# A spectral filter beside a gated dense block on one core: VectorE's own results in the planner, one chunk's dense part ahead of forward tiles, accumulating transfers moved to other sums

## The chip, the core and the metric

The kernel runs on one core of a Trainium2 chip. Work is issued on TensorE (PE in the profile), VectorE (DVE), ScalarE (ACT), GpSimd (POOL, here only a queue that issues accumulating DMAs) and SyncE (SP, the queue of all other DMAs). The metric is the device time of one execution in microseconds (us), as the median of several runs; one further execution was profiled.

## The reference

`x` is 2048 x 512 (the second input `B_x` of the same shape is not used; both parts read `A_x`). Everything is float32.

```python
g = sigmoid((x * gate_w).sum(-1, keepdims=True))          # one gate per row
X = rfft2(x, axes=(-2, -1)) * (w_r + 1j * w_i)            # filter in the frequency domain
a = irfft2(X, s=(2048, 512), axes=(-2, -1))
h = gelu(x @ w1 + b1)                                     # 512 -> 1792
b = h @ w2 + b2                                           # 1792 -> 512
out = g * a + (1 - g) * b
```

## The kernel before, in words

Every product on TensorE is made in split precision: an operand is stored as a rounded high part (suffix `h`) and the remainder (suffix `l`), and a product takes three matmuls, high by high, high by low, low by high. The high part is a copy on ScalarE. The remainder comes in one of two ways: VectorE subtracts the high part from the source (`split`), or ScalarE writes the negated high part into the low buffer and a DMA issued by GpSimd adds the source onto it in place (`minus`, `acc`). VectorE's subtraction of a 128x512 tile and the accumulating DMA of 256 KB are thus two prices for the same thing.

The work falls into these stages:

- **Forward, 16 tiles** (`forward(j)`, rows j, j+16, ...). Per tile: folds on VectorE (`eo`, `w`), a split (`eoh`, `eol`), eight matmuls into `pd`, another split into `zb` buffers (`zb0`/`zb2` high, `zb1`/`zb3` low, used in turn), six matmuls into `py` with a table `tf` loaded for each tile, and a rearrangement into the spectrum `y` by way of `pys`. The gate's logits come out of `pd` as well.
- **Dense block, four chunks of 512 rows, in two halves of the hidden units** (`mlp(half, c)`). Per hidden tile f: twelve 512-wide matmuls into `ph` (names `ph<chunk>_<f>`), gelu on ScalarE, a split into `g<chunk>_<f>h` and `...l`. Then four output tiles `po<half>_<chunk><q>` of 21 matmuls each. Half 0 (f from 0 to 6) stores its sums with the bias in a DRAM buffer `bacc`; half 1 (f from 7 to 13) adds to it. Before the change, chunk 0 of half 0 writes gelu's result to an SBUF tile `gst`, from which ScalarE makes both the high part and the negated one, and an accumulating DMA the low part. The two PSUM tiles that `ph` may hold at a time are then free as soon as gelu has read them.
- **Filter** (`stage1`, `own_rows`, `filt`, `stage4`): radix-4 steps over the 16 tiles and the product with the filter `wf`, almost all on VectorE. `own_rows` sends two rows of the spectrum through DRAM (`ywas`, `own`, `yfix`) and TensorE (`pown`) and comes before the first filter step, whose tiles are `b0d`, `b0s`.
- **Inverse** (`inverse(c, h, late)`): per tile a twist on ScalarE and VectorE (`sw`, `pq`), a split `v`, matmuls into `pz`, a split into `zb`, matmuls into `pa`, then `od`, `u`, `v`, `w`. For the chunks in `LATE` (3 and 0) half 1 of the dense block is already in `bacc`, added there by accumulating DMAs; `inverse` loads it as `ba`, multiplies by the gate and subtracts it from `w` on VectorE before the store. For chunks 1 and 2 the last sum is made in `last`.

The order of the instructions on each engine is fixed when the program is built. `Graph.schedule` is a list planner: each step has an engine, a cost, a lag until its result is there, and a rank, and at each moment the free engine takes the ready step of the lowest rank for which buffers are free. For steps of the same engine (`own`) the planner counts the result as there when the engine is free again, with no lag. `turn_of(n)` is the rank 0.8 + 0.01 n; `EARLY` is 0.5, `FEED` is 1. Forward tiles have ranks from 0.80 to 0.95 in the order `NORD` = 0, 4, 8, 12, 1, 5, ..., 11, 15; tile 15 is the last.

Of the kernel before, what the change touches and what calls it, by code (L numbers as in the profile page):

```python
# [12 lines left out]
F32R = mybir.dt.float32r  # L13
# [42 lines left out]
def _tables():  # L56
# [123 lines left out]
class Graph:  # L180
# [45 lines left out]
    def schedule(self):  # L226
# [123 lines left out]
def tile_kernel(ctx: ExitStack, tc: tile.TileContext, xt, xc, w1, w2, b1, b2, x0g, wf, wrev, out, consts):  # L350
# [204 lines left out]
    def load_mx(half, c):  # L555
        if (half, c) == (1, 3):
            X[half, c] = X[0, 3]
            return
        X[half, c] = new_x(half, c)
        if half == 0:  # L560
            h, l = X[0, c]
            for q in range(NQ):
                def part(b, q=q):
                    return b.ap()[:, q].rearrange("p a b -> p (a b)")

                x = buf("xm", [P, 4 * P], F32, f"xm{c}{q}")
# [12 lines left out]

    def forward(j):  # L580
# [54 lines left out]
        def segs(t, c, lo, step):  # L635
            o = t.ap()[:, c, lo:lo + P]
            return bass.AP(tensor=o.tensor, offset=o.offset, ap=[list(o.ap[0]), [step, 2], list(o.ap[1])])

        for c in range(2):
            a(lambda c=c: act.activation(segs(xh, c, 0, P + c), segs(ps, c, P, P + 4), AF.Copy), 256, [(ps, c)], [(xh, c)], 0)  # L640
# [201 lines left out]
    def inverse(c, h, late):  # L842
# [76 lines left out]
        for k, op in enumerate((ALU.add, ALU.subtract)):  # L919
# [9 lines left out]
            if late:  # L929
                v(lambda w=w, k=k: vec.tensor_tensor(w.ap(), w.ap(), ba[k].ap(), op=ALU.subtract), 512, [ba[k]], [w])  # L930
# [14 lines left out]
    def load_w(n, f):  # L945
# [5 lines left out]
        a(lambda: act.activation(h.ap(), t.ap(), AF.Copy), 512, [t], [h], rank)  # L951
        if f < FA and (n == "a" or f < 0):
            v(lambda: vec.tensor_tensor(l.ap(), t.ap(), h.ap(), op=ALU.subtract), 512, [t, h], [l], rank)
# [3 lines left out]
    def mlp(half, c):  # L957
# [7 lines left out]
        for f in fs:  # L965
# [25 lines left out]
            else:  # L991
                m(up, 512, 12, [*W["a", f], *xx], [ps])
            if half == c == 0:
                t = buf("gst", [P, 512], F32, f"gs{c}_{f}")
                h, l = G[f] = [buf("hid", [P, 512], F32R, f"g{c}_{f}{k}") for k in "hl"]
                rank = 0.9 if half else FEED if c else EARLY
                a(lambda f=f, ps=ps, t=t: act.activation(t.ap(), ps.ap(), AF.Gelu_apprx_tanh, bias=b1t.ap()[:, f:f + 1]), 600,
# [7 lines left out]
            if half and c == 2:  # L1005

                v(lambda ps=ps: vec.scalar_tensor_tensor(ps.ap(), gb.ap()[:, c], 1.0, ps.ap(), op0=ALU.subtract, op1=ALU.mult),
                  512, [gb], [ps], 0.9)
            G[f] = split(f"g{c}_{f}", "hid", [P, 512], ps, lambda x: x, 512, 0.9 if half else FEED if c else EARLY)
        for q in range(NQ):  # L1010
# [16 lines left out]
            for n in (slice(0, 2 * P), slice(2 * P, 4 * P)) if end else (slice(0, 4 * P),):  # L1027
# [142 lines left out]
```

## Time and profile before

| | us |
|---|---|
| median of 3 runs (lowest, highest) | 390.63 (390.21, 390.88) |
| the profiled execution | 391.24 |
| its span, first to last instruction | 389.4 |
| TensorE busy, 1839 matmuls | 374.5 (96%) |
| VectorE busy, 743 instructions | 340.5 (87%) |
| ScalarE busy, 421 instructions | 229.8 (59%) |
| granted TensorE clock | 1.00 |

The profiled execution took 1.84 us more than its span, and 0.61 us more than the median of the runs. Busy time is the union of an engine's instructions. A matmul's record overlaps the next one's, so that short waits between matmuls do not show as idle time: of TensorE's waits the table above shows a part.

### The profile page before, as it was taken

The numbers are of one execution on the slowest core, as the hardware profiler recorded it, in microseconds if no ns is written. First come the engines' busy times: TensorE is split into PE (matmuls) and PEld (weight loads), VectorE is DVE, ScalarE is ACT, GpSimd is POOL, SyncE is SP. The second block draws the span as 40 slices with busy tenths as digits, with TensorE's granted clock in tenths as the row PEclk, the third lists the DMA queues.
The fourth block names the chain that finished last, engine by engine and source line by source line (L and its number), as shares of the span: only waits on it lengthen the run. The fifth ranks groups of instructions, "written<-read, shape, count | busy, mean of one in ns | idle before, by whom it ended". The sixth has DMA issues, their size and how long they took to land.

```text
span 389.4 us, 5547 instructions
## 1 busy us (share of the span) xinstructions
PE 374.5 (96%) x1839; PEld 311.6 (80%) x1839; DVE 340.5 (87%) x743; ACT 229.8 (59%) x421; POOL 32.3 (8%) x52
## 2 busy tenths in 40 slices
PE   8898899999999999999999899999999999998996
PEld 7777788788888888888887677887888878887885
DVE  4999999999998999999979967786979799899962
ACT  4999986688552532375396495379419994045300
POOL 0122320000000000012043002000110000000000
PEclk9999999999999999999999999999999999999999
DMA  8998999966483235669299335416243065610321
GB/s 275 346 279 176 252 241 286 368 213 210 148 264 113 81 135 155 174 162 247 83 247 167 85 159 93 63 36 228 35 63 27 8 222 174 212 43 0 114 105 54
DMA packets 41189, 61.72 MB, mean 158 GB/s; under 512 B 4576, under 2 KB 19488, under 8 KB 40384
## 3 DMA queue, kind: packets, MB, share of 16 engines
q1 hardware_dynamic: 35832, 51.67, 40.2%
q0 software_dynamic: 5184, 9.44, 15.7%
q10 hardware_dynamic: 144, 0.26, 0.3%
q8 instruction: 14, 0.23, 0.2%
q14 instruction: 15, 0.12, 0.1%
HBM read 42.60 MB, written 16.92 MB: 153 GB/s over the span
## 4 chain that ended last, share of the span: by engine, by line
PE 38%; DVE 30%; ACT 19%; DMA 8%; issue 4%; SPq 0%; DVEq 0%; ACTq 0%
PE po L419 20%; PE ph L419 12%; ACT sw L858 4%; DVE m L817 4%; DMA wf<-in_wf 2%; DVE y L721 2%; ACT ph L1003 2%; PE pa L419 2%; DMA bb<-bacc 2%; PE pd L419 2%; ACT sw L861 2%; ACT y L673 2%; DMA ti<-ti 1%; PE pz L419 1%; PE py L419 1%
## 5 line engine op out<-in xcount | busy, mean ns | idle before, releaser
L1003 ACT ACTIVATE ph<-ph,b1t 128x512 f32<-128x512 f32 x49 | 32.1, 656 | 36.6 <-PE ph L419 36.5
L1040 ACT ACTIVATE o<-po,b2t 128x512 f32<-128x512 f32 x16 | 10.9, 691 | 28.5 <-PE po L419 24.9
L858 ACT ACTIVATE sw<-y,al 64x512 f32<-64x512 f32 x32 | 23.1, 723 | 2.6 <-DVE y L721 2.0
L817 DVE TENSOR_TENSOR m<-y,wf 128x514 f32<-128x514 f32 x32 | 20.7, 689 | 0.2
L419 PE MATMUL py<-zb,tf 128*128 128x258 f32 x96 | 17.7, 297 | 3.3 <-ACT pys L666 1.2
L419 PEld LDWEIGHTS py<-zb,tf 128*128 128x128 f32 x96 | 14.3, 189 | 6.5 <-ACT pys L666 1.8
L884 ACT ACTIVATE zb<-pz 128x512 fp32r<-128x512 f32 x16 | 9.4, 592 | 13.5 <-PE pz L419 13.5
L865 DVE SCALAR_TENSOR_TENSOR pq<-y,al,sw 128x256 f32<-128x256 f32 x32 | 14.1, 479 | 3.2 <-ACT sw L861 3.1
L673 ACT ACTIVATE y<-pys 64x257 f32<-64x257 f32 x32 | 13.4, 418 | 4.4 <-DVE pys L670 4.0
L419 PEld LDWEIGHTS pa<-zb,ci 128*128 128x128 f32 x96 | 13.2, 189 | 2.8 <-ACT zb L884 1.6
L419 PE MATMUL pa<-zb,ci 128*128 128x256 f32 x96 | 14.4, 286 | 0.3 <-ACT zb L884 0.2
L642 DVE TENSOR_TENSOR zb<-pd,zb 128x256 fp32r<-128x256 f32 x32 | 12.1, 419 | 2.3 <-ACT zb L640 1.9
L885 DVE TENSOR_TENSOR zb<-pz,zb 128x512 fp32r<-128x512 f32 x16 | 11.0, 685 | 3.0 <-ACT zb L884 3.0
L410 POOL DMA_DIRECT2D bacc<-o x8 | 7.0, 876 | 75.3 <-ACT o L1043 53.0
L593 DVE TENSOR_TENSOR w<-eo 128x256 f32<-128x256 f32 x32 | 12.8, 419 | 0.3
L419 PE MATMUL pd<-cf,eoh 128*128 128x254 f32 (+1 forms) x64 | 10.9, 290 | 1.7 <-ACT eoh L598 1.7
L590 DVE TENSOR_TENSOR eo<-xf 128x256 f32<-128x256 f32 x32 | 12.3, 419 | 0.0
L646 DVE TENSOR_TENSOR zb<-zb,pd 128x256 fp32r<-128x256 f32 (+1 forms) x32 | 11.9, 412 | 0.4
L600 DVE TENSOR_TENSOR eol<-w,eoh 128x512 fp32r<-128x512 f32 (+1 forms) x17 | 11.1, 655 | 1.0 <-ACT eoh L598 1.0
L598 ACT ACTIVATE eoh<-w 128x512 fp32r<-128x512 f32 (+1 forms) x17 | 10.2, 600 | 2.9 <-DVE w L593 2.8
L887 DVE TENSOR_TENSOR zb<-zb,pz 128x512 fp32r<-128x512 f32 x16 | 11.0, 686 | 0.4
L419 PEld LDWEIGHTS pd<-cf,eoh 128*128 128x128 f32 x64 | 9.2, 189 | 2.6 <-ACT eoh L598 1.9
(574 smaller groups left out, 1292.9 us busy)
## 6 DMA issues: line engine op xcount, KB each, us to landing
wf<-in_wf SPq DMA_DIRECT2D x16, 257.0 KB, 3.5
tf<-tf SPq DMA_DIRECT2D x16, 256.0 KB, 5.4
bacc<-o SPq DMA_DIRECT2D x16, 256.0 KB, 3.4
xf<-in_xt SPq DMA_DIRECT2D x15, 256.0 KB, 4.2
war<-in_w SPq DMA_DIRECT2D x14, 256.0 KB, 4.1
wbr<-in_w SPq DMA_DIRECT2D x14, 256.0 KB, 4.4
xm<-in_xc SPq DMA_DIRECT2D x12, 256.0 KB, 3.6
bb<-bacc SPq DMA_DIRECT2D x8, 256.0 KB, 4.9
```

The source lines that it names most:

```text
L419: pe.matmul(ps, w, x, start=start, stop=stop)
L590: v(lambda s=s, op=op: vec.tensor_tensor(eo.ap()[:, s], x.ap()[:, 0:2], x.ap()[:, 2:4], op=op), 256, [x], [(eo, s)], feed)
L593: v(lambda s=s, op=op: vec.tensor_tensor(w.ap()[:, s], eo.ap()[:, :, 0], eo.ap()[:, :, 1], op=op), 256, [eo], [(w, s)], feed)
L600: v(lambda k=k: vec.tensor_tensor(l.ap()[:, k], w.ap()[:, k], h.ap()[:, k], op=ALU.subtract), 256 * len(ps), sub[0] + sub[1], sub[2], feed)
L642: v(lambda c=c: vec.tensor_tensor(segs(xl, c, 0, P + c), segs(ps, c, P, P + 4), segs(xh, c, 0, P + c), op=ALU.subtract), 256, [(ps, c), (x ...
L646: v(lambda o=o, i=i: vec.tensor_tensor(xl.ap()[:, :, o], xl.ap()[:, :, o], ps.ap()[:, :, i], op=ALU.add), 256, [ps], [xl], 0)
L673: a(lambda o=o, i=i: act.activation(Y[j].ap()[o:o + HP, 1], pys.ap()[i:i + HP, 1], AF.Copy), 257, [(pys, 1)], [(Y[j], 1 + k)], 0, more=0.1)
L817: v(lambda mk=mk, k=k, y=y, w=w: vec.tensor_tensor(mk.ap(), y.ap(), w.ap()[:, k:k + 1, :ND].to_broadcast([P, 2, ND]), op=ALU.mult), 514, [ ...
L858: a(lambda sw=sw, y=y, o=o, i=i: act.activation(sw.ap()[o:o + HP], y.ap()[i:i + HP, ::-1, :HD], AF.Copy, scale=al.ap()[i:i + HP, 0:1]), 51 ...
L865: v(lambda sw=sw, pq_=pq_, y=y, j=j, k=k, op=op: vec.scalar_tensor_tensor(pq_.ap()[:, k], y.ap()[:, k, :HD], al.ap()[:, 1 + j:2 + j], sw.a ...
L885: v(lambda n=n, ps=ps: vec.tensor_tensor(zl.ap()[:, :, :, n], ps.ap()[:, :, :, :P], zh.ap()[:, :, :, n], op=ALU.subtract), 512, [ps, (zh, ...
L1003: a(lambda f=f, ps=ps: act.activation(ps.ap(), ps.ap(), AF.Gelu_apprx_tanh, bias=b1t.ap()[:, f:f + 1]), 600, [b1t], [ps], 0.9 if half else ...
```

## The change

The change has six parts; the first two only change the order.

1. In `schedule`, VectorE is taken out of the engines whose own results are there at once: a VectorE step that reads another VectorE step's result now becomes ready only after that step's lag (0.12).
2. Ranks: the input tiles of chunk 1 and weights of half 0 move ahead, and the hidden tiles of chunk 1 get `EARLY` in place of `FEED`, so that they stand ahead of forward tiles.
3. Chunk 0 of half 0 goes the way of the other chunks: gelu in place in PSUM, high part on ScalarE, low part by VectorE's subtraction (7 subtractions more on VectorE, 7 negated copies and 7 accumulating DMAs fewer). The low parts of four weight tiles (`wa3` to `wa6`) go the other way (4 subtractions fewer, 4 negated copies and accumulating DMAs more).
4. For chunks 3 and 0 the dense sums are kept negated (`nb2`, `scale=-1.0`), and the last sum `w` plus `ba` is made by an accumulating DMA from SBUF to SBUF, ahead of the store (8 subtractions fewer on VectorE, 8 accumulating DMAs more).
5. The table `tf` has 192 columns for a split part in place of 256: 16 loads of 192 KB in place of 256 KB.
6. The access pattern of `segs` is written in another way, and the first subtraction for `zb` waits for both halves of the high part.

```diff
-                    own = [q for q in s.after if q.eng == e in ("pe", "vec", "act")]
+                    own = [q for q in s.after if q.eng == e in ("pe", "act")]
...
-    b2t = one("b2t", [P, NQ])
+    b2t, nb2 = one("b2t", [P, NQ]), one("nb2", [P, NQ])
...
-                dma(lambda q=q, x=x: sp.dma_start(x.ap(), xc[c, q]), 256, [], [x], turn_of(8+0.5*q - 2) if c == 1 else FEED)
+                dma(lambda q=q, x=x: sp.dma_start(x.ap(), xc[c, q]), 256, [], [x], turn_of(6+0.5*q - 2) if c == 1 else FEED)
...
-        t = buf("ttab", [P, 2, 2, P], F32R, f"tf{j}")
-        dma(lambda: raw(t.ap(), tf_d[j]), 256, [], [t], feed)
+        t = buf("ttab", [P, 2, 3 * HP], F32R, f"tf{j}")
+        dma(lambda: raw(t.ap(), tf_d[j]), 192, [], [t], feed)
...
-                v(lambda w=w, k=k: vec.tensor_tensor(w.ap(), w.ap(), ba[k].ap(), op=ALU.subtract), 512, [ba[k]], [w])
+                acc(lambda w=w: w.ap(), lambda k=k: ba[k].ap(), 256, [ba[k]], [w])
...
-        return turn_of(8+0.5*f if n == "b" else f-1) if f or n == "b" else EARLY
+        return turn_of(8+0.5*f if n == "b" else 0.57*f-1.6) if f or n == "b" else EARLY
...
-        if f < FA and (n == "a" or f < 0):
+        if f < 3 and (n == "a" or f < 0):
...
-            if half == c == 0:
+            if 0:
...
-            G[f] = split(f"g{c}_{f}", "hid", [P, 512], ps, lambda x: x, 512, 0.9 if half else FEED if c else EARLY)
+            G[f] = split(f"g{c}_{f}", "hid", [P, 512], ps, lambda x: x, 512, 0.9 if half else EARLY if c<2 else FEED)
...
-                a(lambda o=o, ps=ps: act.activation(o.ap(), ps.ap(), AF.Copy), 512, [ps], [o], 2)
+                a(lambda o=o, ps=ps: act.activation(o.ap(), ps.ap(), AF.Copy, scale=-1.0), 512, [ps], [o], 2)
```

What this does to the order is shown at three places. On PE, around the end of the forward stage (`ph1_*` and `po0_100` belong to chunk 1 of the dense block, `pd11`, `pd15`, `py11*`, `py15*` to the last two forward tiles). Before:

```order
L419 MATMUL ph1_1_1212<-mxh01_262,wa1h_190 128x512
...
L419 MATMUL py110_1242<-zb2_91,tf11_1060 128x258 x2
L419 MATMUL py111_1247<-zb2_91,tf11_1060 128x258 x2
...
L419 MATMUL ph1_2_1263<-mxh01_262,wa2h_246 128x512
...
L419 MATMUL py150_1299<-zb1_83,tf15_1129 128x258
L419 MATMUL py151_1302<-zb1_83,tf15_1129 128x258
L419 MATMUL ph1_3_1309<-mxh01_262,wa3h_251 128x512
...
L419 MATMUL po0_100_1338<-g1_0h_1232,wb0h_323 128x512
```

And after, on PE at the same forward tiles:

```order
L421 MATMUL ph1_5_1258<-mxh01_252,wa5h_310 128x512
...
L421 MATMUL ph1_6_1297<-mxh01_252,wa6h_377 128x512
...
L421 MATMUL py110_1322<-zb2_91,tf11_1154 128x258 x2
L421 MATMUL py111_1328<-zb2_91,tf11_1154 128x258 x2
...
L421 MATMUL po0_100_1351<-g1_0h_1046,wb0h_389 128x512
...
L421 MATMUL py150_1369<-zb1_83,tf15_1186 128x258
L421 MATMUL py151_1372<-zb1_83,tf15_1186 128x258
```

The last forward tile used to stand behind three hidden tiles of chunk 1; now it stands behind all seven and twelve matmuls of the first output tile.

On ACT, at the start (`wa*` are weight tiles, `mxh` is the dense block's input, `eoh0` and `zb2` belong to forward tile 0, `gs0_0` is the SBUF tile that falls away). Before:

```order
L951 ACTIVATE wa1h_190<-war1_131 128x512
L598 ACTIVATE eoh0_201<-w0_196 128x256
L997 ACTIVATE gs0_0_207<-ph0_0_147,b1t_121 128x512
L999 ACTIVATE g0_0h_213<-gs0_0_207 128x512
L1000 ACTIVATE g0_0l_235<-g0_0h_213 128x512
L598 ACTIVATE eoh0_201<-w0_196 128x256
L951 ACTIVATE wa2h_246<-war2_135 128x512
L951 ACTIVATE wa3h_251<-war3_152 128x512
L598 ACTIVATE eoh4_256<-w4_240 128x512
```

And after, on ACT from the same instruction on:

```order
L953 ACTIVATE wa1h_190<-war1_131 128x512
L1005 ACTIVATE ph0_0_147<-ph0_0_147,b1t_121 128x512
L468 ACTIVATE g0_0h_208<-ph0_0_147 128x512
L953 ACTIVATE wa2h_227<-war2_135 128x512
L601 ACTIVATE eoh0_233<-w0_198 128x256 x2
L953 ACTIVATE wa3h_240<-war3_152 128x512
L474 ACTIVATE wa3l_246<-wa3h_240 128x512
L571 ACTIVATE mxh01_252<-xm10_168 128x512
```

Gelu works in place, the copies for forward tile 0 stand behind two more copies of the dense block, and the negated copy is now one of a weight.

On DVE, in the first filter step (`b0*`, `m*`, `y` belong to the filter, `g2_*l` to chunk 2 of the dense block). Before:

```order
L717 TENSOR_TENSOR b0s0_1592<-y_362 128x514
L717 TENSOR_TENSOR b0s1_1597<-y_362 128x514
L717 TENSOR_TENSOR y_362<-b0s1_1597,b0s0_1592 128x514
L719 TENSOR_TENSOR y_362<-b0s0_1592,b0s1_1597 128x514
L717 TENSOR_TENSOR y_362<-b0d1_1590,b0d0_1585 128x2x257
L719 TENSOR_TENSOR y_362<-b0d0_1585,b0d1_1590 128x2x257
L817 TENSOR_TENSOR m1_0_1622<-y_362,wf0_1276 128x514
L817 TENSOR_TENSOR m2_0_1637<-y_362,wf0_1276 128x514
L819 TENSOR_TENSOR y_362<-m1_0_1622,m2_0_1637 128x257
```

And after, on DVE in the same filter step:

```order
L719 TENSOR_TENSOR b0s0_1674<-y_348 128x514
L469 TENSOR_TENSOR g2_3l_1678<-ph2_3_1638,g2_3h_1676 128x512
L719 TENSOR_TENSOR b0s1_1680<-y_348 128x514
L719 TENSOR_TENSOR y_348<-b0s1_1680,b0s0_1674 128x514
L721 TENSOR_TENSOR y_348<-b0s0_1674,b0s1_1680 128x514
L469 TENSOR_TENSOR g2_4l_1700<-ph2_4_1660,g2_4h_1698 128x512
L721 TENSOR_TENSOR y_348<-b0d1_1658,b0d0_1656 128x2x257
L819 TENSOR_TENSOR m1_0_1703<-y_348,wf0_1349 128x514
```

Instructions of the dense block now stand between filter instructions that read each other's results, and the filter step comes later among them: `g2_0l`, `g2_1l` and `g2_2l` stand ahead of `b0d0`, where before only chunk 1 did.

More of the change, by code (lines that the diff above doesn't have):

```diff
@@ L96, in _tables @@
     ang = _angle(np.arange(HP), a, j)
-    tf = np.stack([np.concatenate([np.cos(ang), np.sin(ang)], 2), np.concatenate([np.sin(ang), np.cos(ang)], 2)], 2)
-    tf[:, :, :, 0] = 1.0
-    tf[:, :, :, HP] = (1.0 - 2.0 * (a % 2))
+    tf = np.concatenate([np.cos(ang), np.sin(ang)], 2)
+    tf[:, :, 0] = 1.0
+    tf[:, :, HP] = (1.0 - 2.0 * (a[..., 0] % 2))
+    tf = np.concatenate([tf, tf[:, :, :HP]], 2)
     tf = np.stack(_split(tf), 2)
@@ L118, in _tables @@
                 y[r, c] = 0.5
-                u = (y[0, 0] - y[1, 1]) + 1j * (y[0, 0] + y[1, 1])
-                v = ((y[1, 0] - y[0, 1]) + 1j * (y[1, 0] + y[0, 1])) * -1j * np.exp(1j * np.pi * n / NJ)
+                u = (y[0, 0] - y[1, 1]) + 1j * (y[1, 0] + y[0, 1])
+                v = ((y[1, 0] - y[0, 1]) + 1j * (y[0, 0] + y[1, 1])) * -1j * np.exp(1j * np.pi * n / NJ)
                 for q in range(4):
@@ L527, in load_small @@
         dma(lambda: sp.dma_start(b2t.ap(), b2), 2, [], [b2t])
+        add("vec", 0.1, 0.1, lambda: vec.tensor_scalar(nb2.ap(), b2t.ap(), -1.0, None, op0=ALU.mult), [b2t], [nb2], 3)
         dma(lambda: sp.dma_start(rev.ap(), wrev), 32, [], [rev])
@@ L566, in load_mx @@
                 x = buf("xm", [P, 4 * P], F32, f"xm{c}{q}")
-                dma(lambda q=q, x=x: sp.dma_start(x.ap(), xc[c, q]), 256, [], [x], turn_of(8+0.5*q - 2) if c == 1 else FEED)
-                a(lambda part=part, x=x: act.activation(part(h), x.ap(), AF.Copy), 512, [x], [(h, q)], turn_of(8+0.5*q) if c == 1 else FEED)
+                dma(lambda q=q, x=x: sp.dma_start(x.ap(), xc[c, q]), 256, [], [x], turn_of(6+0.5*q - 2) if c == 1 else FEED)
+                a(lambda part=part, x=x: act.activation(part(h), x.ap(), AF.Copy), 512, [x], [(h, q)], turn_of(6+0.5*q) if c == 1 else FEED)
                 if c in ():
-                    minus(h, l, part, 512, lambda q=q: xc[c, q], ([(h, q)], [(l, q)]), turn_of(8+0.5*q) if c == 1 else FEED)
+                    minus(h, l, part, 512, lambda q=q: xc[c, q], ([(h, q)], [(l, q)]), turn_of(6+0.5*q) if c == 1 else FEED)
                 else:
                     v(lambda part=part, x=x: vec.tensor_tensor(part(l), x.ap(), part(h), op=ALU.subtract), 512, [x, (h, q)],
-                      [(l, q)], turn_of(8+0.5*q) if c == 1 else FEED)
+                      [(l, q)], turn_of(6+0.5*q) if c == 1 else FEED)
             if c != 3:
@@ L635, in segs @@
         def segs(t, c, lo, step):
-            o = t.ap()[:, c, lo:lo + P]
-            return bass.AP(tensor=o.tensor, offset=o.offset, ap=[list(o.ap[0]), [step, 2], list(o.ap[1])])
+            return t.ap()[:, c, lo:lo + 2 * step].rearrange("p (a b) -> p a b", a=2)[:, :, :P]
         for c in range(2):
@@ L642, in forward @@
             v(lambda c=c: vec.tensor_tensor(segs(xl, c, 0, P + c), segs(ps, c, P, P + 4), segs(xh, c, 0, P + c), op=ALU.subtract),
-              256, [(ps, c), (xh, c)], [(xl, c)], 0)
+              256, [(ps, c), xh], [(xl, c)], 0)
         for o, i in ((slice(0, P), slice(0, P)), (slice(P + NX, 2 * P), slice(3 * P + NX, 4 * P))):
@@ L656, in s_high @@
             for k in range(2):
-                mm(py[c].ap()[:, :NE], t.ap()[:, k, c], xh.ap()[:, c, :NE], k == 0, False)
+                mm(py[c].ap()[:, :NE], t.ap()[:, k, c * HP:c * HP + P], xh.ap()[:, c, :NE], k == 0, False)
         def s_low(c):
-            mm(py[c].ap()[:, :NE], t.ap()[:, 0, c], xl.ap()[:, c, :NE], False, True)
+            mm(py[c].ap()[:, :NE], t.ap()[:, 0, c * HP:c * HP + P], xl.ap()[:, c, :NE], False, True)
         for c in range(2):
@@ L992, in mlp @@
                 m(up, 512, 12, [*W["a", f], *xx], [ps])
-            if half == c == 0:
+            if 0:
                 t = buf("gst", [P, 512], F32, f"gs{c}_{f}")
                 h, l = G[f] = [buf("hid", [P, 512], F32R, f"g{c}_{f}{k}") for k in "hl"]
-                rank = 0.9 if half else FEED if c else EARLY
+                rank = 0.9 if half else EARLY if c<2 else FEED
                 a(lambda f=f, ps=ps, t=t: act.activation(t.ap(), ps.ap(), AF.Gelu_apprx_tanh, bias=b1t.ap()[:, f:f + 1]), 600,
@@ L1039, in mlp @@
             if half == 0:
-                a(lambda o=o, ps=ps, q=q: act.activation(o.ap(), ps.ap(), AF.Identity, bias=b2t.ap()[:, q:q + 1]), 600,
-                  [b2t, ps], [o])
+                neg = c in LATE
+                a(lambda o=o, ps=ps, q=q, neg=neg: act.activation(
+                    o.ap(), ps.ap(), AF.Identity, bias=(nb2 if neg else b2t).ap()[:, q:q + 1], scale=-1.0 if neg else 1.0), 600,
+                  [nb2 if neg else b2t, ps], [o])
             elif c in LATE:
-                a(lambda o=o, ps=ps: act.activation(o.ap(), ps.ap(), AF.Copy), 512, [ps], [o], 2)
+                a(lambda o=o, ps=ps: act.activation(o.ap(), ps.ap(), AF.Copy, scale=-1.0), 512, [ps], [o], 2)
                 acc(lambda q=q: bacc[c].ap()[:, q].rearrange("p a b -> p (a b)"), lambda o=o: o.ap(), 256, [o],
```

## The prediction

> **What bounds the kernel now.** I read the page, then TensorE's busy time by stage, its waits, and the chain.
>
> ```profile
> span 389.4 us, 5547 instructions
> PE 374.5 (96%) x1839; PEld 311.6 (80%) x1839; DVE 340.5 (87%) x743; ACT 229.8 (59%) x421; POOL 32.3 (8%) x52
> 0.00:20.00 20.00, 17.23 (x83) 14.47 (x84) 13.63 (x40) 13.85 (x27) 2.55 (x18) 1.00 0.93 311
> 20.00:96.00 76.00, 71.84 (x396) 60.74 (x394) 71.99 (x194) 63.35 (x139) 10.50 (x12) 1.00 0.89 253
> 96.00:200.00 104.00, 104.00 (x461) 86.03 (x460) 100.69 (x198) 49.66 (x81) 6.96 (x8) 1.00 0.56 161
> 200.00:224.00 24.00, 22.63 (x98) 17.70 (x97) 20.78 (x43) 15.52 (x28) 5.28 (x6) 1.00 0.72 153
> 224.00:370.00 146.00, 143.01 (x721) 118.90 (x720) 124.94 (x251) 87.41 (x150) 7.00 (x8) 1.00 0.37 98
> ```
>
> The stage rows give length, then busy time of PE, PEld, DVE, ACT and POOL, granted clock, DMA share, GB/s. TensorE is the bound, full from 96 to 200 and idle before and after. Its waits up to 95 us, then those from 200 us (us in total, times, longest):
>
> ```profile
> PE pd L419 <- ACT eoh L598: 1.7, 1, 1.7
> PE py L419 <- ACT pys L666: 1.2, 2, 0.7
> PE py L419 <- DVE pys L670: 1.1, 1, 1.1
> ...
> PE pz L419 <- DVE zb L887: 2.2, 2, 1.6
> PE po L419 <- DVE g_12l L467: 0.6, 1, 0.6
> PE po L419 <- DVE g_10l L467: 0.4, 1, 0.4
> ```
>
> Busy time hides short waits, so I count what TensorE must do and at what pace it does it when nothing is late. The chain and the timeline (start, us, what) give the paces:
>
> ```profile
> 82.36 0.92 PE pd L419 x8
> 104.59 16.36 PE po L419 x72
> 246.20 0.95 PE pa L419 x8
> L419 PE MATMUL none<-zero x12: 628/628/795, 1.1 to 5.9; 128*128 128x512 f32 x12
> 89.82 0.88 PE L419 MATMUL py<-zb,tf 128*128 128x258 f32 x6
> 385.79 0.42 DVE o L1060
> ```
>
> A 512-wide matmul takes 16.36/72 = 0.227 us, one of about 256 columns 0.95/8 = 0.119, a forward tile's eight `pd` 0.92, the twelve warming ones 5.2. Up to the last `py15` the order has 192 of the first, 120 of the second, 16 tiles of `pd` and the warming: 43.7 + 14.3 + 14.7 + 5.2 = 77.9. They end at 89.82 + 6 x 0.119 = 90.5 and began at 1.1, so 11.5 us are lost there. Behind it come 1119 and 268 matmuls, 254.3 + 31.9 = 286.2, which end by 385.8: 9.1 lost, of which the stage rows show 1.4 (200 to 224) and 3.0 (224 to 370) as idle. TensorE thus loses 20.6 of 389.4 us; 3.6 more are the tail behind the last matmul. Only these can be won, since the change leaves TensorE's matmuls as they are.
>
> **Why the forward stage loses.** Counted in the order from behind `pd4`'s logit to `pd15`'s, VectorE has 139 instructions of about 256 columns, 26 of 512, 16 small. Its pace:
>
> ```profile
> 97.42 0.69 DVE L719 TENSOR_TENSOR a1d<-y 128x514 f32<-128x514 f32 x1
> 98.03 1.29 DVE L717 TENSOR_TENSOR a1s<-y 128x514 f32<-128x514 f32 x2
> 99.36 0.69 DVE L717 TENSOR_TENSOR y<-a1s,a1s 128x514 f32<-128x514 f32 x1
> 99.97 0.69 DVE L719 TENSOR_TENSOR y<-a1s,a1s 128x514 f32<-128x514 f32 x1
> ```
>
> Neighbours that do not read each other start 0.61 apart (97.42 to 98.03, 99.36 to 99.97), before the first has ended. The instruction at 99.36 reads what the one before it wrote: that one began at 98.03 + 0.60 = 98.63, so this pair is 0.73 apart. A dependent neighbour costs 0.12 more. By width I take 0.60 and, in proportion with the 0.08 fixed part, 0.335: 46.6 + 15.6 + 1.3, and 16 dependent pairs 1.9, make 65.4 us. TensorE has 168, 90 and 14 tiles from `py40` to the last `py15`: 38.1 + 10.7 + 12.9 = 61.7. VectorE needs more than TensorE, so TensorE waits.
>
> **The change, part by part.**
>
> *Forward stage.* VectorE now has 134, 32, 14 and 18 pairs there: 44.9 + 19.2 + 1.1 + 2.1 = 67.3. TensorE has 60 matmuls more (hidden tiles and the first output tile of chunk 1): 61.7 + 13.6 = 75.3. TensorE needs 8 us more than VectorE, and so sets the pace. Where it starts from is set by ScalarE, whose order begins:
>
> ```profile
> 9.89 0.63 ACT L951 ACTIVATE wa1h<-war 128x512 fp32r<-128x512 f32 x1 [2.73 <-DMA war<-in_w]
> 15.47 0.67 ACT L997 ACTIVATE gs<-ph,b1t 128x512 f32<-128x512 f32 x1
> 16.04 0.64 ACT L640 ACTIVATE zb<-pd 128x256 fp32r<-128x256 f32 x2
> 16.57 0.63 ACT L999 ACTIVATE g_1h<-gs 128x512 fp32r<-128x512 f32 x1
> ```
>
> A gelu takes 0.57, a 512-wide copy 0.53, a 256-wide one 0.27, start to start. From `wa1h` (9.89) to the first half of `zb0`, which `py40` waits for, the order now has 13 copies, 3 gelus and 6 short copies: 6.9 + 1.7 + 1.6 = 10.2, so 20.1, and I add 0.3 for `war5`'s landing: 20.4 (before: row 19.9, 0.119 x 6 behind 19.18). Then 75.3, and 2 for waits (0 at best; at worst 5.2, which VectorE lost in the stage of before, 90.5 - 19.9 - 65.4): `py15` ends at 97.7. The same work before: 90.5 + 13.6 = 104.1. **Gain 6.4** (3.2 to 8.4).
>
> Of the parts in it: seven subtractions more and four fewer on VectorE are in the counts; the negated copies, three fewer, are in ScalarE's. The low parts of `wa3` to `wa6` now come by accumulating DMA:
>
> ```profile
> DMA to landing us min/median/max: 3.9/5.1/8.0
> bacc<-o POOLq DMA_DIRECT2D x8, 256.0 KB, 4.2
> ```
>
> `wa3l`'s is issued at about 13.8 and lands by 22 even at 8.0; TensorE wants it at 20.4 + 0.24 + 0.45 = 21.1. I take the median, 18.9, nothing lost; at 8.0 it costs 0.7. GpSimd's queue has nothing ahead of it but the other weights. Gelu in place holds one of the two PSUM tiles of `ph` through a copy and a subtraction more (0.53 + 0.60, and VectorE's queue), so `ph0_4` waits for `g0_2l`. TensorE has `ph0_3` and forward pieces in between, over 4 us: nothing. The smaller `tf` takes 1 MB from a stretch where DMA share is 0.93 and 0.89; I give it nothing.
>
> *Filter stage.* The first filter step now stands behind `g2_2l`, which needs `ph2_2`: 108 matmuls behind `py15`, 97.7 + 24.7 = 122.4, and 1.9 for gelu, copy and subtraction: 124.3. Before:
>
> ```profile
> 116.87 1.30 DVE L719 TENSOR_TENSOR b0d<-y 128x514 f32<-128x514 f32 x2 [0.17 <-DMA y<-yfix]
> 224.09 0.69 DVE L467 TENSOR_TENSOR g_13l<-ph,g_13h 128x512 fp32r<-128x512 f32 x1 [0.56 <-ACT g_13h L466]
> L930 DVE TENSOR_TENSOR w<-w,ba x8: 683/692/693, 321.4 to 370.8; 128x512 f32<-128x512 f32 x8
> ```
>
> From `b0d0` to chunk 3's `g3_13l` VectorE had 127, 60, 20 and 34 dependent pairs, 103.5 us, in 107.8 (224.7 - 116.87): 4.3 of waits. Now 108, 52, 19 and 8 pairs: 85.7. With the same waits it ends at 214.3; TensorE wants `g3_13l` behind 519 matmuls, at 97.7 + 118 = 215.7 with small ones left out. It just holds. Before, it came 2 us late. I count 0.5 lost: **gain 1.5** (2 at best; with double the waits, a loss of 1).
>
> [...]
>
> *Inverse and end.* The eight subtractions of the L930 row go, 8 x 0.60 = 4.8 on VectorE, as do 19 dependent pairs, 2.3. Where VectorE was late in this stage:
>
> ```profile
> 354.04 0.68 DVE L885 TENSOR_TENSOR zb<-pz,zb 128x512 fp32r<-128x512 f32 x1
> 354.75 0.69 DVE L887 TENSOR_TENSOR zb<-zb,pz 128x512 fp32r<-128x512 f32 x1
> 355.58 1.19 PE pz L419 x8
> ```
>
> The wait of 1.6 is a queue on VectorE with a dependent pair at its end. The stage loses about 7; I take **a gain of 1.5**. At best 4; at worst a loss of 2, if buffers of `w` held through two transfers make VectorE wait. At the end three accumulating DMAs and loads follow each other: `w100`'s adding frees `ba101`'s buffer, `ba101` is loaded and scaled, `w101`'s adding, the store. Counted back from the last matmul with 4.2 each, `w101` lands some 2 us ahead of the last output tile: nothing. At 8.0 each it would cost 5.
>
> On SP the store of each `w` now waits for its adding, and holds what is queued behind. The nearest is `ti12`, behind `ba000`, whose buffer `w031`'s adding frees. That adding is issued about when `ph2_8` ends; from there to `pz12` TensorE has 63 and 28 matmuls, 17.6 us, and adding, load and scaling take 4.2 + 4 or so (8.0 + 4 at worst): nothing. GpSimd's queue has only chunk 0's additions ahead, long done. `nb2` is one instruction of four columns.
>
> *Sum.* 6.4 + 1.5 + 1.5 = 9.4. The profiled span goes to 380.0, its execution (391.24, 1.84 above the span) to 381.8, and the median of runs (390.63) to **381.2**.
>
> **The rivals.**
> - *The filter stage becomes late* (15%). For it: VectorE starts it 7 us later and my slack is 1.4. If it waits 8.6 in place of 4.3 and the inverse then hangs on it, the gain of the last two parts turns into a loss of about 1: 385. Against it: 18 us of VectorE work have moved behind `g3_13l`.
> - *Transfers set the early pace* (8%). For it: DMA share 0.93. Then the new order can't run faster than loads come, and only 1.5 + 1.5 is left: 387.6. Against it: of the waits up to 95 us, none of the large ones names a DMA.
> - *Slower, by PSUM* (7%). Two `ph` tiles are held until VectorE subtracts. If VectorE reaches each subtraction of chunks 0 and 1 later than TensorE has other work, TensorE stops at twelve hidden tiles; from 0.8 us each on it eats the whole gain (12 x 0.8 = 9.6), at 1.2 the time is 395. Against it: VectorE's 8 us of slack.
> - *The 0.12 is not the dependence's* (3%): then the 26 pairs resolved in the filter stage save nothing, VectorE ends it 26 x 0.12 = 3.1 later, 1.7 beyond my slack: 382.9. The four rows of VectorE's pace speak against it. [...]
> - *It does nothing* (4%): each gain turns into a wait elsewhere, 390.6.
> - *More is won* (5%): early 8.4, late 6: 376.
> - The forecast, 379 to 384: 58%.
>
> **How the numbers follow.** Faster: 58 + 15 + 8 + 3 + 5 = 89%; same (within 0.2%, about what a measurement of this kernel tells from nothing) 4%; slower 7%. The range 377 to 387.3 leaves out the slower, the unchanged, most of the transfers' case and of the best one, some 2 in 10.
>
> **What would show it.** TensorE's idle time from 20 to 96 us falls from 4.2 to about 2, with `py15` ending near 98. VectorE starts `b0d` near 124. Waits for `g_10l` to `g_12l` are gone. `zb` in L887's successor releases `pz` with less than 1 us. The last store is still that of `o`, not `w`. I am wrong if ScalarE's early order holds TensorE beyond 21 us at `py40`, if VectorE idles for transfers around `b0d`, or if `w`'s stores end the program.

## The result, and the profile after

The changed kernel takes 380.99 us (median of 6 runs, 379.32 to 382.74), the kernel before 390.68 beside it (6 runs): a ratio of 0.9737, 95% interval 0.9683 to 0.979. The forecast was 381.2. The profiled execution took 379.32 us, with a span of 377.6, the shortest of the six.

The page's head and engine line, and the stage rows (length, busy time of PE, PEld, DVE, ACT, POOL, granted clock, DMA share, GB/s):

```profile
span 377.6 us, 5551 instructions
PE 368.8 (98%) x1839; PEld 311.2 (82%) x1839; DVE 335.3 (89%) x739; ACT 228.8 (61%) x418; POOL 36.6 (10%) x57
0.00:20.00 20.00, 17.32 (x82) 14.18 (x82) 13.86 (x42) 14.17 (x28) 2.55 (x18) 1.00 0.91 280
20.00:96.00 76.00, 74.43 (x413) 63.84 (x414) 69.09 (x181) 59.76 (x131) 7.83 (x9) 1.00 0.77 221
96.00:200.00 104.00, 104.00 (x463) 86.13 (x463) 98.58 (x201) 57.07 (x94) 8.20 (x10) 1.00 0.64 183
200.00:224.00 24.00, 24.00 (x108) 19.87 (x107) 22.48 (x47) 9.33 (x17) 5.75 (x7) 1.00 0.83 183
224.00:370.00 146.00, 145.23 (x748) 123.56 (x747) 130.12 (x270) 88.50 (x150) 12.22 (x14) 1.00 0.40 103
```

TensorE's idle time is a stage's length less PE's busy time. It falls from 4.16 to 1.57 us between 20 and 96, from 1.37 to nothing between 200 and 224, and from 2.99 to 0.77 behind that. TensorE's waits between 20 and 96 us, and those from 200 us on (us in total, times, longest):

```profile
PE py L421 <- ACT zb L642: 1.5, 2, 1.4
PE ph L421 <- DMA wa3l<-in_w: 0.7, 1, 0.7
...
PE pz L421 <- DVE zb L889: 0.8, 2, 0.5
```

One line is left of the late waits; those for `g_10l` to `g_12l` are gone. The places that the forecast named, from the timeline (start, us, what): `py40`, the wait for `wa3l`, the last `py15`, `b0d0`, chunk 3's `g3_13l` and the matmul that reads it, the last matmul, the last store; then the median landing of `wa3l`'s DMA:

```profile
20.76 0.52 PE L421 MATMUL py<-zb,tf 128*128 128x258 f32 x2 [1.39 <-ACT zb L642]
22.39 0.50 PE L421 MATMUL ph<-mxh,wa3l 128*128 128x512 f32 x1 [0.66 <-DMA wa3l<-in_w]
99.11 0.40 PE L421 MATMUL py<-zb,tf 128*128 128x258 f32 x2
126.28 1.29 DVE L721 TENSOR_TENSOR b0d<-y 128x514 f32<-128x514 f32 x2
215.43 0.69 DVE L469 TENSOR_TENSOR g_13l<-ph,g_13h 128x512 fp32r<-128x512 f32 x1 [0.22 <-ACT g_13h L468]
216.85 0.39 PE L421 MATMUL po<-g_13l,wb13h 128*128 128x512 f32 x1
373.57 0.28 PE L421 MATMUL po<-g_13h,wb13l 128*128 128x256 f32 x1
374.34 0.33 SPq L1069 DMA_DIRECT2D out<-o  x1
wa3l<-in_w POOLq DMA_DIRECT2D x1, 256.0 KB, 8.0
```

By the forecast's own count: the last `py15` ends at 99.11 + 2 x 0.119 = 99.35. Before, the same work (with the 60 matmuls that now stand ahead of it) would have ended at 104.1, so 4.75 us are won up to there. Behind it stand 286.2 - 13.6 = 272.6 us of matmuls, and the last ends at 373.57 + 0.12 = 373.69: 1.7 us are lost there. For the kernel before, the last matmul and the ones that read `g_13l` (the first at 225.2) are:

```profile
385.47 0.28 PE L419 MATMUL po<-g_13h,wb13l 128*128 128x256 f32 x1
L419 PE MATMUL po<-g_13l,wb13h x17: 283/389/398, 225.2 to 385.4; 128*128 128x512 f32 x15, 128*128 128x256 f32 x2
```

So its last matmul ended at 385.59. The prediction took 385.8, which is VectorE's start behind it; by the same measure as now, 8.9 us were lost behind `py15` and not 9.1, and the tail was 3.9 and not 3.6. That makes 7.15 us won behind `py15`, and the tail stays at 3.9. 4.75 + 7.15 = 11.9 is the distance between the two spans (389.4 and 377.6), but for a rounding.

The 7.15 can be divided at the first matmul that reads chunk 3's `g_13l`. Before, 580 wide and 4 narrow matmuls, 132.3 us of work, stood between the last `py15` and it, and took 225.2 - 90.53 = 134.7. Now it is 517 and 2, 117.7 us, and they take 216.85 - 99.35 = 117.5. So 2.4 us were lost there and nothing is now (the -0.2 is the error of the count): about 2.6 won. The other 4.5 lie behind it.

### The profile page after: what moved, and what is told of

Same layout as the page of the kernel before. It is cut to its first block, busy times and chain, and to the rows that moved or that the text cites. A ratio compares the mean times of both kernels' runs of the same rounds, so it can differ in the third digit from the quotient of the medians.

```text
span 377.6 us, 5551 instructions
## 1 busy us (share of the span) xinstructions
PE 368.8 (98%) x1839; PEld 311.2 (82%) x1839; DVE 335.3 (89%) x739; ACT 228.8 (61%) x418; POOL 36.6 (10%) x57
## 4 chain that ended last, share of the span: by engine, by line
PE 78%; ACT 10%; DMA 6%; DVE 5%; issue 1%; SPq 0%
PE ph L421 35%; PE po L421 32%; ACT sw L860 3%; PE pz L421 3%; PE pa L421 3%; PE pd L421 3%; PE py L421 2%; DMA wa3l<-in_w 2%; ACT sw L863 2%; DMA xm<-in_xc 1%; DMA war<-in_w 1%; ACT ph L1005 1%; DMA xf<-in_x0g 1%; DVE y L723 1%; ACT zb L886 0%
## 5 line engine op out<-in xcount | busy, mean ns | idle before, releaser
L1005 ACT ACTIVATE ph<-ph,b1t 128x512 f32<-128x512 f32 x56 | 36.9, 659 | 42.6 <-PE ph L421 42.3
L421 PE MATMUL py<-zb,tf 128*128 128x258 f32 x96 | 16.9, 288 | 1.5 <-ACT zb L642 1.5
L421 PEld LDWEIGHTS py<-zb,tf 128*128 128x128 f32 x96 | 14.8, 189 | 4.1 <-ACT zb L642 1.9
L412 POOL DMA_DIRECT2D w<-ba x8 | 7.0, 901 | 75.4 <-DVE w L929 42.2
L1048 ACT ACTIVATE o<-po 128x512 f32<-128x512 f32 x8 | 4.7, 596 | 14.5 <-PE po L421 14.5
L1044 ACT ACTIVATE o<-po,b2t 128x512 f32<-128x512 f32 x8 | 5.5, 690 | 13.0 <-PE po L421 12.2
L412 POOL DMA_DIRECT2D wa7l<-in_w x1 | 0.9, 881 | 116.1 <-ACT wa7l L474 116.1
L1044 ACT ACTIVATE o<-po,nb 128x512 f32<-128x512 f32 x8 | 5.4, 689 | 10.9 <-PE po L421 10.9
L642 ACT ACTIVATE zb<-pd 128x256 fp32r<-128x256 f32 x32 | 10.5, 383 | 2.0 <-PE pd L421 1.7
```

What stands on the lines that cost most here:

```text
L412: return add("pool", 2.3 * kb / 340, 3.4, lambda: nc.gpsimd.dma_start(dst(), src(), accum_op=ALU.add), reads, writes, rank)
L421: pe.matmul(ps, w, x, start=start, stop=stop)
L1005: a(lambda f=f, ps=ps: act.activation(ps.ap(), ps.ap(), AF.Gelu_apprx_tanh, bias=b1t.ap()[:, f:f + 1]), 600, [b1t], [ps], 0.9 if half else ...
```

## The experiments

All times are medians; each ratio is to the kernel before, run on the same chip in the same set. My theory after the result was that the early gain comes from the ranks, and that VectorE's relief (the planner's rule on its own results, and the last sums) carries the rest. The rivals were that one of these alone does everything, that transfers or the held PSUM tiles set the pace, and that a dependent neighbour costs VectorE nothing.

**The rule undone in the changed kernel.**

```diff
-                    own = [q for q in s.after if q.eng == e in ("pe", "act")]
+                    own = [q for q in s.after if q.eng == e in ("pe", "vec", "act")]
```

> Changed kernel with the planner's rule alone undone: VectorE's own last result is again taken as free, so the planned order has 90 dependent neighbours on VectorE in place of 45, 32 in place of 8 between b0d0 and g3_13l. Theory (VectorE's relief carries the gain behind 200 us): the early part stays (py15 ends near 99), VectorE needs 98.4 us in place of 85.7 from b0d0 to g3_13l, TensorE waits again for g_1xl and later: 384 to 386 us. Rival (dependent neighbours cost nothing that TensorE feels; the moved rows carry everything): 380.5 to 381.5.

383.72 us, ratio 0.9845 (0.9821 to 0.987). It is slower than the changed kernel, a little less than the theory said, and only half of it where it said: TensorE's idle time is 2.97 us from 20 to 96, 0.36 from 200 to 224, and only 0.53 behind 224. Counted by matmuls as above, 1.8 of the 3.6 us between the two spans are lost ahead of the end of the last `py15`, and 1.8 behind it. Without the rule the planner puts 204 matmuls of 512 columns between `py40` and the last `py15` in place of 228: two hidden tiles fewer.

**The rule alone, in the kernel before** (the same line, the other way).

> Kernel of before with the planner's rule alone changed (dependent neighbours 92 to 40; ranks, loads and last sums as before). Theory: about half of the gain, from the stage of the forward tiles (VectorE 62.9 us of work against 65.4) and from the end: 385 to 387. Rival (the rule carries all): 381. Rival (it carries nothing): 390.5.

386.46 us, ratio 0.99 (0.9876 to 0.9923), as the theory's number has it. The place is again another one: from 20 to 96 TensorE idles 4.65 us, no less than before. The gain is behind 200: 0.86 and 1.19 where 1.37 and 2.99 were.

**The ranks undone.**

```diff
-                dma(lambda q=q, x=x: sp.dma_start(x.ap(), xc[c, q]), 256, [], [x], turn_of(6+0.5*q - 2) if c == 1 else FEED)
+                dma(lambda q=q, x=x: sp.dma_start(x.ap(), xc[c, q]), 256, [], [x], turn_of(8+0.5*q - 2) if c == 1 else FEED)
...
-        return turn_of(8+0.5*f if n == "b" else 0.57*f-1.6) if f or n == "b" else EARLY
+        return turn_of(8+0.5*f if n == "b" else f-1) if f or n == "b" else EARLY
...
-            G[f] = split(f"g{c}_{f}", "hid", [P, 512], ps, lambda x: x, 512, 0.9 if half else EARLY if c<2 else FEED)
+            G[f] = split(f"g{c}_{f}", "hid", [P, 512], ps, lambda x: x, 512, 0.9 if half else FEED if c else EARLY)
```

> Changed kernel with the ranks of before (chunk 1's hidden tiles behind the forward tiles, chunk 1's rows from tile 8 on, weights by f-1); VectorE's rule, accumulating DMAs and small tables stay. Theory (the early gain of 4.5 us is TensorE's extra 60 matmuls): most of it is lost, 384 to 386. Rival (VectorE's shorter queue alone does it, the ranks are idle): 381.

386.78 us, ratio 0.9916 (0.9893 to 0.994). The ranks are needed: TensorE idles 4.88 us from 20 to 96, and 0.41 behind 224. Part of the time is the granted clock's (last section): its mean is 0.984 to 0.991 in five of the six executions. The sixth, at 0.999, took 384.78, so some 4 us are lost at full clock too.

**The last sums on VectorE again.**

```diff
-                acc(lambda w=w: w.ap(), lambda k=k: ba[k].ap(), 256, [ba[k]], [w])
+                v(lambda w=w, k=k: vec.tensor_tensor(w.ap(), w.ap(), ba[k].ap(), op=ALU.subtract), 512, [ba[k]], [w])
```

(with the negation of `o` and `b2` taken back too)

> Changed kernel with the eight last sums of the late chunks as VectorE subtractions again (order up to chunk 3 of the second half unchanged). Theory (late stage gained by VectorE's relief): 4.8 us more on VectorE, half of which TensorE feels: 382.5 to 383.5, with waits of pz for zb. Rival (VectorE has room late and the sums could have stayed): 380.5 to 381.5.

381.14 us, ratio 0.9782 (0.975 to 0.9815). The interval overlaps the changed kernel's, so a price of 0 to 2 us is all that it shows. The trace puts most of it at the end: the last matmul starts at 374.82 in place of 373.57, and the span ends 5.0 us behind it in place of 4.0. Of the 1.25 us between the two starts, 0.4 are there already at the last `py15` (99.78 in place of 99.35), ahead of everything that this edit touches.

**The changed kernel once more.**

> The changed kernel once more, unchanged, as the yardstick for the runs beside it. Theory (the spread of its times is the granted clock of TensorE, which halves for some microseconds in some executions): spans near 377.6 wherever the mean clock is above 0.998, and about half a microsecond more for each 0.001 to 0.002 that the clock is lower; median 380 to 381.5. Rival (the spread has nothing to do with the clock): spans of 377.6 to 381 at any clock.

380.11 us, ratio 0.9741 (0.9703 to 0.9779). The pairs of span (us) and mean granted clock were 377.0 at 0.998, 378.2 to 378.5 at 0.994 and 0.995, and 379.0 at 1.000. The last fits the rival and not the theory, so the clock is a part of the spread and not all of it.

**`wa3`'s low part on VectorE.**

```diff
-        if f < 3 and (n == "a" or f < 0):
+        if f < 4 and (n == "a" or f < 0):
```

> Changed kernel with the low part of wa3 made by a VectorE subtraction again (wa4 to wa6 stay accumulating DMAs). Theory (the changed kernel loses 0.7 us at ph2_3 because that accumulating DMA took 8.0 us among the first loads): the wait for wa3l goes, 0.3 to 0.8 us faster than the changed kernel: about 380. Rival (VectorE, which has no spare time before tile 4, is late elsewhere by as much): as the changed kernel or 1 us slower.

382.64 us, ratio 0.9801 (0.9765 to 0.9837): slower than the changed kernel beside it by 2.5, where a gain was expected. Its waits from 20 to 96:

```profile
PE py L421 <- DVE pys L672: 1.3, 1, 1.3
PE ph L421 <- DMA wa4l<-in_w: 1.3, 1, 1.3
```

With one input changed the planner wrote another order. `ph0_4` stands earlier in it and meets `wa4l` on its way; VectorE, loaded by one more subtraction, is late at `pys`. The 0.7 us at `wa3l` were the smaller evil. Not all of the loss is there: TensorE idles 3.05 us in this stage in place of 1.57, and 1.57 behind 224 in place of 0.77.

**The full tables.**

```diff
-    tf = np.concatenate([tf, tf[:, :, :HP]], 2)
+    tf = np.concatenate([tf, tf], 2)
...
-        t = buf("ttab", [P, 2, 3 * HP], F32R, f"tf{j}")
+        t = buf("ttab", [P, 2, 4 * HP], F32R, f"tf{j}")
```

> Changed kernel with every instruction in its place, but each of the 16 table loads tf 256 KB again in place of 192 KB (1 MB more, most of it before 60 us). Theory (no long wait of TensorE names a load): within 0.5 us of the changed kernel. Rival (transfers set the early pace): 1 MB at about 300 GB/s is 3.5 us, so 383 to 384.5.

379.61 us, ratio 0.9723 (0.9683 to 0.9763). With every instruction in its place, 1 MB more costs nothing that can be measured (380.11 us without it, in the same set). The volume of the loads does not set the early pace here.

**Chunk 0's gelu copied out of PSUM again.**

```diff
-            if 0:
+            if half == c == 0:
                 t = buf("gst", [P, 512], F32, f"gs{c}_{f}")
```

> Changed kernel with chunk 0's hidden tiles again copied out of PSUM (gelu to a buffer, copy, negated copy, accumulating DMA) in place of gelu in place and a VectorE subtraction. Theory: chunk 0's seven tiles cost ScalarE 7 x 0.53 us more and VectorE 7 x 0.60 us less in the stage where ScalarE's order already holds TensorE at py40; slower by 1 to 3 us: 382 to 384. Rival (PSUM tiles held through the subtraction were what the changed kernel pays): faster, 379 to 380.

391.79 us, ratio 1.0031 (1.0003 to 1.0059): the whole gain is gone with this one part. Neither theory nor rival had it. The granted clock has a share in the number (0.983 to 0.991 in eleven of the twelve executions), but the twelfth, at 0.996, took 389.85, which leaves no gain either. The stage row from 20 to 96 us, and TensorE's largest waits in it:

```profile
20.00:96.00 76.00, 67.86 (x373) 57.57 (x373) 68.08 (x182) 62.62 (x139) 12.18 (x14) 0.98 0.92 259
PE py L421 <- ACT pys L668: 2.3, 2, 1.7
PE py L421 <- PE py L421: 1.9, 2, 1.0
PE py L421 <- ACT zb L642: 1.9, 1, 1.9
PE po L421 <- ACT gs L999: 1.3, 1, 1.3
```

8.1 us idle where the changed kernel has 1.6. In this order the planner finds only 168 of the 512-wide matmuls to put between `py40` and the last `py15`, as in the kernel before, where the changed one has 228. Behind its matmuls each hidden tile of chunk 0 goes through four steps in place of three, the last an accumulating DMA that lands 5.0 to 6.8 us behind its issue, and so its output tiles and chunk 1's hidden tiles come later. That these steps hold chunk 1 back is read from the order and not tried by itself.

**That part alone, in the kernel before** (the same line, the other way).

> Kernel of before with one part of the change alone: chunk 0's gelu in place in PSUM and a VectorE subtraction, without the ranks, the rule, the sums and the small tables. Theory (the two ph tiles are held until VectorE subtracts, and with the old ranks VectorE comes to it behind the forward tiles): TensorE finds only 38.7 us of work between py40 and the last py15 (59.1 before, 72.8 in the changed kernel) while VectorE has 66 us; the 20 us left over are added behind: 400 to 408 us. Rival (gelu in place is a gain by itself, as it frees ScalarE of 14 instructions): 386 to 389.

426.7 us, ratio 1.0919 (1.0889 to 1.0949): the direction and the size's order are the theory's, and the loss is greater than it said. The profiled execution took 962.83 us, more than twice the others' 425.44 to 427.19, so no time of its trace is read. The order of its instructions is fixed when the program is built, and can be counted: 78 of the 512-wide matmuls stand between `py40` and the last `py15`, where the kernel before has 168. In the other executions the mean granted clock is 0.952 to 0.955; by my estimate 0.046 x 424.6 = 19.5 us is the most that this can have cost, and 426.7 less that is 407, within the theory's range. So the thinner order is shown. That it comes from PSUM tiles held for VectorE, as the theory has it, was not tried by itself.

**That part and the ranks, in the kernel before.** Without the rule and the accumulated sums, with `wa3` to `wa6` on VectorE and the full tables.

> Kernel of before with gelu in place and the ranks, without the rule, the accumulated sums, wa3 to wa6 by DMA, and the small tables. Theory (these two together make the early gain; the late stage stays as before): 4 to 5 us early, little behind 200 us: 384.5 to 387. Rival (the rule on dependent neighbours is needed for any of it): 389 to 391.

382.24 us, ratio 0.9786 (0.9758 to 0.9813): 8.2 of some 10 us, more than the theory said. Part 6 of the change is left out here too; it and the low parts of `wa4` to `wa6` were not tried by themselves. Stage rows from 20 to 96, 200 to 224 and 224 to 370, and its late waits:

```profile
20.00:96.00 76.00, 75.16 (x422) 64.70 (x422) 73.38 (x198) 61.22 (x136) 6.24 (x7) 1.00 0.76 226
200.00:224.00 24.00, 24.00 (x107) 19.73 (x106) 23.51 (x50) 10.55 (x18) 4.55 (x6) 1.00 0.80 177
224.00:370.00 146.00, 142.61 (x724) 119.31 (x723) 129.68 (x265) 84.92 (x147) 5.28 (x6) 1.00 0.33 92
PE pz L419 <- DVE tg L852: 1.5, 1, 1.5
PE pz L419 <- DVE zb L887: 1.3, 1, 1.3
```

The early stage is filled even better than in the changed kernel (0.84 idle), and the filter stage is no longer late, without the rule. Only behind 224 it loses 3.39 us, nearly all to VectorE, as the kernel before does. So these two parts carry the early and the filter stage's gain, and what the others add lies late. The ranks alone, in the kernel before, were not run, nor was it tried which of the ranks matters.

**Rule and last sums both undone.**

> Changed kernel with both the planner's rule and the last sums undone (e1 with the eight sums on VectorE again). Theory (either of the two takes VectorE off the path of the late chunks, so that undoing one alone cost little there): the late loss of 3 to 4 us returns behind 300 us: 386 to 388. Rival (the sums are worth nothing in any company): as e1, 383 to 384.5.

385.03 us, ratio 0.9871 (0.9839 to 0.9904): between the two numbers, and its interval overlaps that of the rule undone alone. Its idle time behind 224 is 1.83 us, with a wait of 1.27 for `zb` in it.

TensorE's idle time from 224 to 370 us in these kernels, from their stage rows, and what is lost from the first matmul that reads chunk 3's `g_13l` to the last one, by the count of matmuls (0.2272 and 0.119 us each), which sees the short waits too:

| rule | last sums by DMA | kernel | idle, us | lost by the count, us |
|---|---|---|---|---|
| no | no | before | 2.99 | 6.5 |
| no | no | gelu and ranks | 3.39 | 6.1 |
| no | no | both undone | 1.83 | 4.2 |
| yes | no | rule alone | 1.19 | 3.2 |
| yes | no | sums undone | 1.08 | 2.9 |
| no | yes | rule undone | 0.53 | 2.5 |
| yes | yes | changed | 0.77 | 2.0 |
| yes | yes | ranks undone | 0.41 | 1.9 |
| yes | yes | gelu copied back | 0.81 | 2.1 |
| yes | yes | `wa3` on VectorE | 1.57 | 3.6 |

With neither, 4.2 to 6.5 us are lost by the count; with one, 2.5 to 3.2; with both some 2 (3.6 in the one kernel whose order changed with `wa3`). Either of the two takes VectorE off most of the late path, and the second finds little left to win, 0.4 to 1.1 us.

**Measured by itself**, behind the end of the changed kernel:

> The changed kernel with measurements behind its end (the time itself means nothing): on VectorE 16 additions of 514 columns that do not read each other, 16 of which each reads the one before, and 16 of which each reads the one before last; on ScalarE 16 copies that do not read each other and 16 that do; on quiet queues 4 accumulating DMAs of 256 KB one after another, 4 plain loads, 4 accumulating DMAs to four places. Theory (only the neighbour's result costs): VectorE 0.61, 0.73 and 0.61 us start to start. Rival (the semaphore costs nothing): 0.61 three times; or 0.73 three times. Accumulating DMAs alone: 3.2 to 4.2 us from issue to landing; if 5 and more, the 8.0 at the start is not the other loads' doing.

The two engines' timelines there (start and length of a whole series of 16):

```profile
374.61 9.75 DVE L1133 TENSOR_TENSOR y<-y 128x514 f32<-128x514 f32 x16
384.28 11.62 DVE L1135 TENSOR_TENSOR y<-y 128x514 f32<-128x514 f32 x16
395.94 9.76 DVE L1137 TENSOR_TENSOR y<-y 128x514 f32<-128x514 f32 x16
405.12 8.53 ACT L1139 ACTIVATE y<-y 128x514 f32<-128x514 f32 x16 [45.51 <-DVE y L1137]
413.56 10.56 ACT L1141 ACTIVATE y<-y 128x514 f32<-128x514 f32 x16
```

On VectorE independent neighbours take (384.28 - 374.61)/16 = 0.604 us each, dependent ones (395.94 - 384.28)/16 = 0.729, and with one instruction between 0.604 again (9.76 as against 9.75 for the series). A dependent neighbour costs 0.125, and one instruction between hides all of it, as the theory had it. The four accumulating DMAs of 256 KB that followed each other took 6.1 (beside the last store), 5.1, 4.3 and 5.2 us to landing, more than the 3.2 to 4.2 expected; the median of all eight, with the four issued together, was 5.3. But the queues were not quiet: the plain loads were issued too, and the DMA share was 0.57 to 0.80 from 376 to 390 us. Late in the changed kernel the additions to `w` landed in 3.2 to 5.1. So how much of the 8.0 of `wa3l` is its own, and how much came with what else was under way, stays open.

## Why the prediction was right

*Time.* 381.2 forecast, 380.99 measured. That close an agreement is luck. The early gain was 1.65 us smaller than said and the two later ones 4.1 larger, so the profiled span came to 377.6 where the sum gave 380.0. And the median of the six lies 1.7 us above the profiled execution, where the forecast had it 0.6 below, as in the kernel before; this takes the 2.4 back.

*TensorE is the bound, and only its 20.6 us of losses can be won.* Held: the tail did not move, and the 11.9 us that the change brought are all out of these losses.

*Forward stage: 6.4 forecast, 4.75 measured, within its 3.2 to 8.4.* `py40` came at 20.76 (20.4). `wa3l` took the upper end of its bounds, 8.0, and cost the 0.7 that stood beside it. From `py40` to the end of the last `py15` TensorE took 78.6 us: 75.3 of work, as counted, and 3.3 of waits where I took 2. The idea that TensorE sets the pace there held: it is busy 74.43 of 76 us. What I had wrong was whose gain it is. I gave the 60 matmuls more to the ranks and put gelu in place down to three copies fewer on ScalarE, with a PSUM risk beside it. The runs show that neither the rest of the change without it, ranks included (391.79), nor it alone without the ranks (426.7) wins anything, and that the two together bring 8.2 us of the gain.

*Transfers.* The rival is out: 1 MB more in the same order changed nothing that can be measured (379.61 us with it, 380.11 without). One transfer's landing did cost its 0.7.

*PSUM.* I priced it at 395 and 7%. Alone in the old ranks gelu in place costs far more than that (426.7), for this reason or another. In the changed kernel no wait between 20 and 96 us names a `ph` tile that VectorE still held.

*Filter stage: 1.5 forecast, about 2.6 measured, beyond the 2 that I gave as the best.* `b0d0` starts at 126.28 (124.3), `g3_13l` ends at 215.43 + 0.69 = 216.12, and TensorE reads it at 216.85 without a wait. It just holds, as forecast, with 0.7 us to spare, and VectorE's time from `b0d0` to there is 89.8 us where I had 90.0. I took a loss of 2 us before and of 0.5 now; they were 2.4 and nothing. The kernel with gelu and ranks alone loses nothing there either, so the moved work does it without the rule; with the rule alone 0.86 us of idle time stay.

*The 0.12 us.* Measured by itself: 0.125. The rival that the 0.12 is not the dependence's is out, and so is the probe's, one pace for all three series: 0.604 us without the dependence, 0.729 with it, 0.604 with one instruction between. The 0.335 that I took in proportion for 256 columns is near what the kernel before shows:

```profile
21.20 0.42 DVE L667 TENSOR_TENSOR y<-py,pys 128x257 f32<-128x257 f32 x1
21.54 0.41 DVE L670 TENSOR_TENSOR pys<-py,pys 128x257 f32<-128x257 f32 x1
```

These two neighbours of 257 columns start 0.34 apart.

*Inverse and end: 1.5 forecast, 4.5 measured, beyond the 4 that I gave as the best.* This is the term that was mis-sized most. I saw 4.8 and 2.3 us of relief on VectorE against 7 lost, and credited a fifth, as if the lateness would move on. The table shows that each relief alone removes most of it. That fits a VectorE that is late by a short queue at a few places, not by its whole load. And `w`'s stores and buffers, for which I kept 2 us of loss, cost nothing that shows: SP waited up to 14.8 us for an addition to `w`, but no wait of TensorE names it, and VectorE waited 0.4 us for `ba`.

*What would show it.* Idle time of 1.57 where I said about 2; `py15` ended at 99.35 where I said near 98; `b0d` 2 us later than said; `g_10l` to `g_12l` gone; the longest wait of `pz` 0.5; the last store that of `o`. All came, the two times some 2 us late.

## What to carry to other kernels

Two parts of a change can each bring nothing or a loss, and be most of the gain together: price them jointly, at the buffer or engine that they hand to each other. (Here it may be the PSUM tiles, which are free only when VectorE has subtracted; the runs show that the two parts need each other, not why.) Where an engine is late at a few places, ask how much relief removes the last late place; further relief is worth little. And with a greedy planner a small change of one input rewrites the order: what moves the time is the new order, so undo a part, alone and together with its neighbours, before crediting it.

## What the runs showed of the hardware

**In three kernels TensorE's granted clock fell to 0.50 to 0.57 behind a stretch of waits.** Their stage rows: the ranks undone, the last sums undone, and gelu copied back (length, busy times, granted clock in the last column but two):

```profile
80.00:84.00 4.00, 2.52 (x18) 1.97 (x16) 3.56 (x10) 2.62 (x7) 0.00 (x0) 1.00 0.45 150
84.00:91.00 7.00, 6.29 (x18) 5.03 (x19) 6.79 (x18) 2.99 (x7) 0.00 (x0) 0.52 0.03 9
```

```profile
18.00:22.00 4.00, 2.38 (x19) 2.08 (x17) 3.48 (x11) 3.82 (x10) 1.73 (x2) 1.00 0.94 264
22.00:26.00 4.00, 4.00 (x13) 3.15 (x13) 3.46 (x10) 3.21 (x6) 1.25 (x3) 0.57 1.09 275
```

```profile
64.00:68.00 4.00, 1.72 (x9) 1.41 (x10) 3.88 (x11) 3.25 (x8) 0.00 (x0) 0.97 0.91 316
68.00:71.00 3.00, 3.00 (x12) 2.63 (x11) 1.41 (x5) 0.78 (x3) 0.00 (x0) 0.50 0.00 0
```

Each time some 1.5 to 2.3 us of waiting within 4 us come first, and then 3 to 7 us at 0.50 to 0.57. In the second, a 512-wide matmul takes 0.43 us from start to start in place of 0.227:

```profile
22.82 0.63 PE L421 MATMUL ph<-mxh,wa3l 128*128 128x512 f32 x1
23.25 0.63 PE L421 MATMUL ph<-mxh,wa3h 128*128 128x512 f32 x1
```

In the first kernel the 7 us at 0.52 are worth up to 7 x 0.48 = 3.4 us of TensorE's time, an estimate from the row, beside the 1.48 us of waits ahead of them. The lower clock need not show in the time: in the second, the stretch from `py40` to the end of the last `py15` took 78.6 us, as in the changed kernel, whose row from 20 to 96 us shows 1.00. Nor does it always follow on waits: the repeated run of the changed kernel waits 2.3 us ahead of `py40` (from 18 to 22 us), and its stage rows up to 370 us all show 1.00. TensorE was not wholly idle in any of the three stretches (1.72 to 2.52 us busy of 4). That the waits bring the lower clock, and that a wait so costs twice, is not shown: no run here was made to test it. Whether the lower clock has a share in what the kernel with gelu alone lost (mean granted clock 0.952 to 0.955) stays open.

**ScalarE has a similar price for a dependent neighbour.** Independent copies start (413.56 - 405.12)/16 = 0.528 us apart, so that one lasts 8.53 - 15 x 0.528 = 0.61; dependent ones start (10.56 - 0.61)/15 = 0.663 apart: 0.135 more. The planner still takes ScalarE's own last result as free; what the rule would bring there was not tried.
